# SwiGLU block on one core: the first loads spread over two queues, ten transfers in place of seven

## The chip, the core and the metric

The kernel runs on one core of a Trainium2 chip. The metric is the device time of the launch in microseconds, as the median of several runs. Five engines take part: TensorE (PE; its weight loads are a row of their own, PEld), VectorE (DVE), ScalarE (ACT), GpSimd (POOL) and SyncE (SP). DMA transfers are issued here from two queues, SyncE's and ScalarE's.

## The reference

All arrays are bf16. x has 2048 rows of 640; w_gate and w_up are 640 x 1536; w_down is 1536 x 640.

```
g = silu(x @ w_gate)
u = x @ w_up
out = (g * u) @ w_down
```

## The kernel before, in words

The rows of x are cut into four blocks of 512 (`NSB`, loop over `sb`). The contraction length 640 is five tiles of 128 (`KD`), and the hidden width 1536 is twelve tiles of 128 (`KF`, loop over `fc`). For each block and each `fc` five matmuls make `pg` (gate) and five make `pu` (up), both in PSUM, with the weights as the stationary side and xT, the transposed x, as the moving one (`proj`, line 132). ScalarE takes the Silu of `pg` (line 178), and VectorE multiplies it by `pu` into `aT` (line 179). After twelve `fc` come the products with w_down: `po_t` (line 187) for the last 128 output columns and four `po_a` (line 211) for the first 512, copied out by ScalarE and stored.

TensorE's instructions for the first block's start are kept in the order of the program (`keep_order`). In that order they are: 18 warm-up matmuls on a tile of ones (line 101); transposes of x chunks 0 and 2 (line 123, five each); 4 more warm-up matmuls; transposes of chunks 1 and 3; 2 warm-up matmuls; the gate product of `fc` 0 in two halves (`proj_pair`, line 147: five matmuls for chunks 0 and 2, then five for chunks 1 and 3); the up product of `fc` 0 (line 132); and then everything else. The copies of the transposed chunks into xT (line 128) are VectorE's for chunks 0 and 2; for chunks 1 and 3 ScalarE copies two of the five tiles and VectorE three. So the second half of the gate product waits for copies by both engines. For the blocks after the first, xT is filled by transposing DMAs (line 95).

The weights are loaded in column slices `W_CHUNKS`: slice 0 is `fc` 0 (160 KB for each of gate and up), slice 1 is `fc` 1 and 2 (320 KB each), and three slices of three `fc` follow (480 KB each). The loads are issued at the head of the program (lines 81 to 95):

- SyncE: x chunk 0 (160 KB); x chunks 1 and 3 as one (320 KB); gate slice 1; up slice 1; then the other slices, w_down, and the three transposing loads.
- ScalarE: x chunk 2; gate slice 0; up slice 0; then the load of the function table and a first Silu on one column (line 87), so that the table is there early. ScalarE's xT copies and all later Silus stand behind these.

No queue is written out for the DMAs; each queue issues in the order of the program. Each load signals its end on one of eight completion counters, which are handed out in turn; a load whose counter was used before waits, on its issuing queue, until that earlier load has landed. In the program before, the first eight loads are the two queues' loads down to SyncE's gate slice 2; its up slice 2 is the first that waits, for x chunk 2.

Of the kernel before, what the change touches and what calls it, by code (L numbers as in the profile page):

```python
# [10 lines left out]
def _body(  # L11
# [8 lines left out]
    nc = tc.nc  # L20
# [12 lines left out]
    KD = D // P  # L33
# [7 lines left out]
    W_CHUNKS = [(0, 1), (1, 3), (3, 6), (6, 9), (9, 12)]  # L41
# [10 lines left out]
    x_sb = consts.tile([P, SUB, D], bf16)  # L52
    xT = consts.tile([P, KD, S], bf16)
    wg_sb = consts.tile([P, KD, F], bf16)
    wu_sb = consts.tile([P, KD, F], bf16)
# [5 lines left out]
    x_v = x2.rearrange("(c p) d -> p c d", p=P)  # L61
    xt_v = x2.rearrange("s (kd p) -> s kd p", p=P)
    wg_v = w_gate.rearrange("(kd p) f -> p kd f", p=P)
    wu_v = w_up.rearrange("(kd p) f -> p kd f", p=P)
    wd_v = w_down.rearrange("(kf p) d -> p kf d", p=P)

    def wslice(a, b):
        return slice(a * P, b * P)

    def load_w(eng, dst, src, a, b):  # L70
        eng.dma_start(out=dst[:, :, wslice(a, b)], in_=src[:, :, wslice(a, b)])  # L71

    def load_x(eng, *chunks):
        c_sl = slice(chunks[0], chunks[-1] + 1, 2)
        eng.dma_start(out=x_sb[:, c_sl, :], in_=x_v[:, c_sl, :])  # L75

    ones = consts.tile([P, P], bf16)
    silu_first = consts.tile([P, 1], f32)
    nc.vector.memset(ones[:], 1.0)  # L79

    load_x(nc.sync, 0)
    load_x(nc.scalar, 2)
    load_x(nc.sync, 1, 3)
    load_w(nc.scalar, wg_sb, wg_v, *W_CHUNKS[0])
    load_w(nc.scalar, wu_sb, wu_v, *W_CHUNKS[0])
    load_w(nc.sync, wg_sb, wg_v, *W_CHUNKS[1])
    nc.scalar.activation(silu_first[:], ones[:, 0:1], ACT.Silu)  # L87
    load_w(nc.sync, wu_sb, wu_v, *W_CHUNKS[1])
    for a, b in W_CHUNKS[2:]:
# [65 lines left out]
    for sb in range(NSB):  # L155
        s_sl = slice(sb * S_BLK, (sb + 1) * S_BLK)
        for fc in range(KF):
# [16 lines left out]
            else:  # L174
# [5 lines left out]
                out=aT[:, fc, s_sl], in0=sg[:], in1=pu[:], op=ALU.mult  # L180
# [17 lines left out]
        for q in range(P // Q):  # L198
            nc.scalar.dma_start(
                out=out2[  # L200
                    sb * S_BLK : sb * S_BLK + n_t, DA + q * Q : DA + (q + 1) * Q
                ].rearrange("(i r) c -> r i c", r=Q),
                in_=ot_q[q * Q : (q + 1) * Q, :].rearrange("r (i c) -> r i c", c=Q),
# [106 lines left out]
def kernel(tc, *args):  # L310
    _body(tc, *args)
    tc.close()
    tc.compile()
    _trim(tc.nc)
# [30 lines left out]
```

## Time and profile before

| | us |
|---|---|
| median of 3 runs | 165.53 (165.24 to 165.65) |
| the profiled execution | 165.53 |
| its span in the profile | 164.2 |
| TensorE busy | 160.9 |
| ScalarE busy | 42.5 |
| VectorE busy | 37.9 |

The profile is of one execution; times within it are us from the span's start. In a timeline, a row is a merged run of like instructions: start, length, engine, line, operation, tiles, count, and in brackets how long the engine sat idle before it and what ended that. PEld is the loading of weights, which runs beside the matmuls. SPq and ACTq are the issues of DMAs, not the transfers: a transfer's own time is given as the time from issue to landing. TensorE is busy for nearly all of the span, so the time is that of its work and of the few places where it waits.

The transfers issued first, with the start of the issue and the median time to landing of their kind (us):

| load | queue | issue | to landing |
|---|---|---|---|
| x chunk 0 | SyncE | 0.00 | 2.5 |
| x chunk 2 | ScalarE | 0.13 | 2.7 |
| x chunks 1 and 3 | SyncE | 0.47 | 3.6 |
| gate slice 0 | ScalarE | 0.56 | 4.9 |
| gate slice 1 | SyncE | 0.91 | 5.6 |
| up slice 0 | ScalarE | 1.04 | 6.5 |
| up slice 1 | SyncE | 1.43 | 6.4 |

### The profile page before, as it was taken

Reading aid. Unit: us, or ns where it says so; the run is one execution under the profiler, and the core shown is the slowest. Engines: PE = TensorE matmul, PEld = TensorE weight load, DVE = VectorE, ACT = ScalarE, POOL = GpSimd, SP = SyncE. Lnnn points to the kernel's source line nnn. Section 1 sums busy time; section 2 is a strip of 40 time slices with the busy share of each in tenths; the row PEclk is TensorE's granted clock in tenths of the full one; section 3 lists DMA queues with packets and bytes.
Section 4 is the critical chain, followed back from the end, with each engine's and each line's share of the span. In section 5 each row is a group of like instructions: output and inputs, shape, how many; then the busy total and the mean of one; then the engine's idle time right before and its main releaser. Section 6 shows DMA issues by size and latency. Waiting matters only on the chain.

```text
span 164.2 us, 1881 instructions
## 1 busy us (share of the span) xinstructions
PE 160.9 (98%) x781; PEld 76.0 (46%) x781; DVE 37.9 (23%) x58; ACT 42.5 (26%) x72; POOL 0.6 (0%) x6
## 2 busy tenths in 40 slices
PE   8899999999999999999999999999999999999994
PEld 8544444444444444444444444444444444445442
DVE  2233332230013333221003333322001333332000
ACT  3312222212142222212232222221214222222121
POOL 1000000000000000000000000000000000000000
DMA  7999999704200000002210000000320000000312
GB/s 214 296 327 332 363 192 213 141 0 66 66 32 0 0 0 0 4 0 26 72 56 8 2 4 0 0 0 0 64 68 32 0 0 0 0 0 4 51 37 72
DMA packets 26840, 11.26 MB, mean 69 GB/s; under 512 B 17616, under 2 KB 26832, under 8 KB 26832
## 3 DMA queue, kind: packets, MB, share of 16 engines
q1 hardware_dynamic: 17296, 10.13, 23.1%
q10 hardware_dynamic: 9536, 1.02, 4.2%
q8 instruction: 6, 0.10, 0.3%
q14 instruction: 2, 0.02, 0.0%
HBM read 6.55 MB, written 2.62 MB: 56 GB/s over the span
## 4 chain that ended last, share of the span: by engine, by line
PE 94%; DMA 4%; ACTq 1%; DVE 0%; issue 0%
PE pu L132 32%; PE pg L132 31%; PE po_a L211 25%; PE po_t L187 6%; DMA wu_sb<-in_w_up_dram 4%; PE po_b L224 0%; ACTq L71 0%; ACTq L75 0%; DVE ot_b L232 0%
## 5 line engine op out<-in xcount | busy, mean ns | idle before, releaser
L132 PE MATMUL pu<-xT,wu_sb 128*128 128x512 bf16 x240 | 59.6, 379 | 0.8 <-DMA wu_sb<-in_w_up_dram 0.8
L132 PE MATMUL pg<-xT,wg_sb 128*128 128x512 bf16 x235 | 58.4, 379 | 0.0
L179 DVE TENSOR_TENSOR aT<-sg,pu 128x512 bf16<-128x512 f32 x48 | 33.0, 688 | 101.7 <-PE pu L132 101.7
L178 ACT ACTIVATE sg<-pg 128x512 f32<-128x512 f32 x48 | 28.7, 597 | 72.4 <-PE pg L132 71.0
L211 PE MATMUL po_a<-wd_sb,aT 128*128 128x512 bf16 x192 | 42.1, 379 | 0.0
L132 PEld LDWEIGHTS <-wu_sb 128*128 128x128 bf16 x240 | 23.4, 98 | 29.1 <-DMA wu_sb<-in_w_up_dram 1.1
L132 PEld LDWEIGHTS <-wg_sb 128*128 128x128 bf16 x235 | 23.0, 98 | 27.7
L211 PEld LDWEIGHTS <-aT 128*128 128x128 bf16 x192 | 18.8, 98 | 22.5
L219 ACT CAST ot<-po_a 128x512 bf16<-128x512 f32 x16 | 9.4, 586 | 32.3 <-PE po_a L211 21.2
L187 PE MATMUL po_t<-aT,wd_sb 128*128 128x512 bf16 (+1 forms) x48 | 10.4, 366 | 0.0
L187 PEld LDWEIGHTS <-wd_sb 128*128 128x128 bf16 x48 | 4.7, 98 | 5.1
L196 ACT CAST ot_t<-po_t 128x512 bf16<-128x512 f32 (+1 forms) x4 | 2.2, 559 | 11.7 <-PE po_t L187 11.7
L197 DVE STREAM_TRANSPOSE ot_q<-ot_t 128x512 bf16<-128x512 bf16 (+1 forms) x4 | 2.7, 678 | 9.1 <-ACT ot_t L196 9.1
L101 PE MATMUL pw<-ones 128*128 128x128 bf16 x24 | 3.2, 313 | 0.4 <-DVE ones L79 0.4
L101 PEld LDWEIGHTS <-ones 128*128 128x128 bf16 x24 | 2.6, 147 | 0.4 <-DVE ones L79 0.4
L232 DVE CAST ot_b<-po_b 128x128 bf16<-128x128 f32 x1 | 0.3, 292 | 9.9 <-PE po_b L224 9.9
L128 DVE COPY xT<-pt 128x640 bf16<-128x640 bf16 (+1 forms) x4 | 1.7, 425 | 3.7 <-PE pt L123 3.6
L123 PE MATMUL pt<-ident,x_sb 128*128 128x128 bf16 x20 | 2.5, 311 | 0.0
L123 PEld LDWEIGHTS <-x_sb 128*128 128x128 bf16 x20 | 2.0, 143 | 0.4 <-DMA x_sb<-in_x_dram 0.3
L87 ACT ACT_TABLE_LOAD x1 | 1.3, 1283 | 1.6 <-issue 1.6
L147 PE MATMUL pg<-xT,wg_sb 128*128 128x256 bf16 x10 | 1.3, 281 | 0.0
L128 ACT COPY xT<-pt 128x256 bf16<-128x256 bf16 x2 | 0.7, 372 | 1.5 <-PE pt L123 1.5
(11 smaller groups left out, 3.8 us busy)
## 6 DMA issues: line engine op xcount, KB each, us to landing
out_dram<-ot SPq DMA_DIRECT2D x16, 128.0 KB, 1.7
wd_sb<-in_w_down_dram SPq DMA_DIRECT2D x1, 1920.0 KB, 12.8
wg_sb<-in_w_gate_dram SPq DMA_DIRECT2D x3, 480.0 KB, 7.9
wu_sb<-in_w_up_dram SPq DMA_DIRECT2D x3, 480.0 KB, 8.0
out_dram<-ot_q ACTq DMA_DIRECT2D x12, 32.0 KB, 1.9
x_sb<-in_x_dram SPq DMA_DIRECT2D x1, 320.0 KB, 3.6
wg_sb<-in_w_gate_dram SPq DMA_DIRECT2D x1, 320.0 KB, 5.6
wu_sb<-in_w_up_dram SPq DMA_DIRECT2D x1, 320.0 KB, 6.4
```

What stands on the lines that cost most here:

```text
L87: nc.scalar.activation(silu_first[:], ones[:, 0:1], ACT.Silu)
L101: nc.tensor.matmul(pw[:, 0:P], lhsT=ones[:], rhs=ones[:], start=True, stop=True)
L123: nc.tensor.transpose(out=pt[:, kd - k0, :], in_=x_sb[:, c, kd * P : (kd + 1) * P], identity=ident[:],)
L128: copy(out=xT[:, k0:k1, c_sl], in_=pt[:])
L132: nc.tensor.matmul(ps[:, c0:c1], lhsT=w_sb[:, kd, fc * P : (fc + 1) * P], rhs=xT[:, kd, sb * S_BLK + c0 : sb * S_BLK + c1], start=(kd == 0 ...
L178: nc.scalar.activation(sg[:], pg[:], ACT.Silu)
L179: nc.vector.tensor_tensor(out=aT[:, fc, s_sl], in0=sg[:], in1=pu[:], op=ALU.mult)
L187: nc.tensor.matmul(po_t[:], lhsT=wd_sb[:, kf, DA:D], rhs=aT[:, kf, sb * S_BLK : sb * S_BLK + n_t], start=(kf == 0), stop=(kf == KF - 1),)
L196: nc.scalar.copy(ot_t[:], po_t[:])
L197: nc.vector.transpose(out=ot_q[:], in_=ot_t[:])
L211: nc.tensor.matmul(po_a[:], lhsT=aT[:, kf, s0 : s0 + P], rhs=wd_sb[:, kf, 0:DA], start=(kf == 0), stop=(kf == KF - 1),)
L219: nc.scalar.copy(ot[:], po_a[:])
```

## The change

The first loads are issued as ten transfers in place of seven. Each x chunk is a transfer of its own, chunks 0 and 1 from SyncE and 2 and 3 from ScalarE. Gate slice 0, up slice 0 and gate slice 1 are each cut along the contraction: SyncE loads tiles 0 to 2 of the five, ScalarE tiles 3 and 4. ScalarE's part of gate slice 1 is issued ahead of the function table's load. Up slice 1 and all that follows stay whole and on SyncE. In the built program the order on TensorE, VectorE and GpSimd is the same as before; ScalarE has two DMAs more and SyncE one, and a matmul group that reads a cut slice waits for SyncE's part at its first matmul and for ScalarE's at its fourth.

The counters, in turn, now go round earlier. In the built program SyncE's part of gate slice 1 waits for x chunk 0, ScalarE's part for x chunk 2, SyncE's up slice 1 for x chunk 3, gate slice 2 for x chunk 1, and the next ones for the parts of gate and up slice 0.

```
-    def load_x(eng, *chunks):
-        c_sl = slice(chunks[0], chunks[-1] + 1, 2)
-        eng.dma_start(out=x_sb[:, c_sl, :], in_=x_v[:, c_sl, :])
+    def load_x(eng, c0, c1):
+        eng.dma_start(out=x_sb[:, c0:c1, :], in_=x_v[:, c0:c1, :])
...
-    load_x(nc.sync, 0)
-    load_x(nc.scalar, 2)
-    load_x(nc.sync, 1, 3)
-    load_w(nc.scalar, wg_sb, wg_v, *W_CHUNKS[0])
-    load_w(nc.scalar, wu_sb, wu_v, *W_CHUNKS[0])
-    load_w(nc.sync, wg_sb, wg_v, *W_CHUNKS[1])
+    queues = (nc.sync, nc.scalar)
+    halves = ((0, KD // 2 + 1), (KD // 2 + 1, KD))
+
+    def load_halves(dst, src, a, b):
+        for eng, (k0, k1) in zip(queues, halves):
+            eng.dma_start(out=dst[:, k0:k1, wslice(a, b)], in_=src[:, k0:k1, wslice(a, b)])
+
+    for c in (0, 1):
+        for i, eng in enumerate(queues):
+            load_x(eng, c + 2 * i, c + 2 * i + 1)
+    load_halves(wg_sb, wg_v, *W_CHUNKS[0])
+    load_halves(wu_sb, wu_v, *W_CHUNKS[0])
+    load_halves(wg_sb, wg_v, *W_CHUNKS[1])
     nc.scalar.activation(silu_first[:], ones[:, 0:1], ACT.Silu)
     load_w(nc.sync, wu_sb, wu_v, *W_CHUNKS[1])
```

## The prediction

> **What bounds the kernel now.** First I read the busy shares and the chain of work that ended last on the page. TensorE is busy all through, and the only long piece of the chain that isn't TensorE is one load:
>
> ```profile
> PE 160.9 (98%) x781; PEld 76.0 (46%) x781; DVE 37.9 (23%) x58; ACT 42.5 (26%) x72; POOL 0.6 (0%) x6
> ...
> PE 94%; DMA 4%; ACTq 1%; DVE 0%; issue 0%
> ```
>
> Then the chain in order of time. It enters TensorE at 7.59 us through a transfer of wu_sb issued at 1.04, and from there only matmuls follow, one group of five every 1.08 us to the end of the block:
>
> ```profile
> 1.04 6.51 DMA wu_sb<-in_w_up_dram
> 7.59 1.25 PE pu L132 x5
> 8.84 1.08 PE pg L132 x5
> ```
>
> So the work after 7.59 is fixed by TensorE, and every tenth that its first full "up" group starts earlier comes off the end, as long as no later load becomes late. The change touches nothing but what lies before that. There I read the timeline between 3.5 and 7.7 us; the bracket on the last row is the stall:
>
> ```profile
> 3.56 0.63 PE L101 MATMUL pw<-ones 128*128 128x128 bf16 x4
> ...
> 4.06 1.25 PE L123 MATMUL pt<-ident,x_sb 128*128 128x128 bf16 x10
> 4.49 0.37 ACT L128 COPY xT<-pt 128x256 bf16<-128x256 bf16 x1 [1.38 <-PE pt L123]
> ...
> 5.10 0.42 PE L101 MATMUL pw<-ones 128*128 128x128 bf16 x2
> ...
> 5.47 1.33 PE L147 MATMUL pg<-xT,wg_sb 128*128 128x256 bf16 x10
> ...
> 7.58 0.76 PEld L132 LDWEIGHTS <-wu_sb 128*128 128x128 bf16 x5 [1.06 <-DMA wu_sb<-in_w_up_dram]
> ```
>
> The waits put three stalls of weight loads down to loads: 1.1 us for wu_sb, 0.2 for wg_sb and 0.3 for x chunk 0. Last, what the DMA engines moved (columns: stretch and its length, then busy time and count of the five engines, the granted clock, the DMA share, GB/s):
>
> ```profile
> 1.00:2.00 1.00, 1.00 (x13) 1.00 (x11) 0.00 (x0) 0.39 (x1) 0.00 (x0) 1.00 0.88 228
> 2.00:3.00 1.00, 0.97 (x10) 0.71 (x9) 0.00 (x0) 0.99 (x2) 0.00 (x0) 1.00 1.03 337
> 3.00:4.00 1.00, 1.00 (x12) 0.93 (x9) 0.68 (x2) 0.11 (x1) 0.00 (x0) 1.00 1.09 290
> 4.00:5.00 1.00, 1.00 (x12) 0.94 (x11) 0.49 (x2) 0.37 (x1) 0.00 (x0) 1.00 1.01 282
> 5.00:6.00 1.00, 1.00 (x10) 0.69 (x9) 0.53 (x2) 0.37 (x1) 0.00 (x0) 1.00 1.11 279
> 6.00:7.00 1.00, 0.81 (x8) 0.48 (x5) 0.00 (x0) 0.15 (x1) 0.00 (x0) 1.00 1.14 282
> ```
>
> The engines are full from about 1.4 us on. Summed, they have moved 565 KB by 3.0 us, 855 by 4.0, 1137 by 5.0, 1416 by 6.0 and 1698 by 7.0. Bandwidth is what is short, so the order of the bytes decides.
>
> **The change, part by part.** *Order of the bytes.* Before, SyncE issues the second gate slice (328 KB) at 0.91, ahead of ScalarE's first up slice (164 KB, 1.04), and the second up slice at 1.43. They share the engines, and the first up slice lands at 1.04 + 6.5 = 7.54, when about 1.85 MB are through. After, everything that comes first goes first: x (655 KB), gate slice 0 (819 in all), up slice 0 (983), then gate slice 1 (1311) and up slice 1 (1638). At the rate of before these sums are through at 3.3, 3.9, 4.5, 5.6 and 6.8 us. From bytes to landing I take 0.75 to 1.05 us: x 1 and 3 landed at 0.47 + 3.6 = 4.07 against 3.3, up slice 1 at 1.43 + 6.4 = 7.83 against 6.8. That gives x 4.1, gate 0 4.6 to 4.9, up 0 5.2 to 5.5, gate 1 6.4 to 6.7, up 1 7.6 to 7.8. If ScalarE's part of gate slice 1 (131 KB) is served ahead of SyncE's part of up slice 0, add 0.5 to up 0: 6.0 at worst.
>
> *What TensorE gains.* Slots of the pairs are (1.33 - 0.27)/9 = 0.12 us on average and 0.11 once the first is through; those of transposes and warm-up matmuls (1.25 - 0.31)/9 = 0.10 to 0.11.
> - Up slice 0: the last pair starts at 5.47 + 1.33 - 0.27 = 6.53, so the up group could start at 6.64 instead of 7.59: **0.94**.
> - Gate slice 0: the second of the two warm-up matmuls starts at 5.10 + 0.42 - 0.31 = 5.21, so the first pair could start at 5.31 instead of 5.47: **0.16**.
> - x: the fourth gap matmul starts at 3.56 + 0.63 - 0.31 = 3.88, so chunk 1 could start at 3.98 instead of 4.06: **0.08**. Chunk 3 now has its own load, but TensorE reaches it five slots later, at 4.5.
> - TensorE's slow start takes something back. Weight loads of the transposes take 151 ns (median), those of the pairs 98; only the first pair matmul is slow, 353 ns beside 273. So the array sped up at about 5.6 us, though the granted clock reads 1.00 in every row. With the pairs from 5.23, one more runs at the slow pace: **-0.12**. Bounds: no slow pair, +0.1; all ten slow (twice 0.107 each from 5.23), the up group starts at 7.37 and only 0.22 is left. I take the row's 5.6.
>
> The Trainium skill, page "TensorE: Matmul & The Clock Gate", section "Part 1: The HAM clock gate", says the speed-up comes after a window of about 3.4 us of activity that runs freely, so its place differs from run to run. The trace has one execution and can't show that spread; by the page the last term could lie anywhere between its two ends.
>
> Sum: 0.94 + 0.16 + 0.08 - 0.12 = **1.06 us**; the up group at about 6.5.
>
> *Three more issues, two in front of the table load.* SyncE's issues take 0.40 to 0.53 us each: x 0, x 1, gate 0 and up 0 end at about 1.9, still 2.5 us before their bytes could be served, so they cost nothing. The program has eight completion counters for loads, handed out in turn; a ninth load waits until the first that used its counter has landed. Before, SyncE's second 480 KB load met this, at no cost (SyncE's waits):
>
> ```profile
> SPq L71 <- DMA x_sb<-in_x_dram: 0.3, 1, 0.3
> ```
>
> After, SyncE's part of gate slice 1 waits for x 0 (2.5), up slice 1 for x 3 (about 4.1), the later ones for gate and up slice 0. Behind these waits stand all SyncE loads, w_down and the transposed x loads; w_down landed at 10.68 + 12.8 = 23.5 and is used at 32.6, so they have room. Up slice 1 is needed at 6.5 + 2 x 1.08 = 8.7 and lands at 7.6 to 7.8. Gate slice 1: needed 7.6, lands 6.4 to 6.7.
>
> ScalarE's part of gate slice 1 waits for x 2, which landed at 0.13 + 2.7 = 2.83. Behind it on ScalarE stand the table load (1.28), the first Silu (0.20) and both xT copies (0.37 each), for which the second half of the pairs waits. With an issue of 0.5: 3.35, table to 4.65, Silu to 4.87, copies to 5.25 and 5.63. The second half of the pairs starts at about 5.95, so 0.3 us of cover are left: **0**. The issue is bounded by 0.40 (the shortest) and 2.26 (the longest of SyncE's, its seventh, with four large loads outstanding). ScalarE then has three small ones outstanding, like SyncE's fourth and fifth issue (0.53): I take 0.5. Every tenth over 0.8 would cost a tenth.
>
> The Trainium skill, page "DMA: Bandwidth & Descriptors", section "Rules for kernel authors", speaks against this change: splitting a transfer over two queues buys nothing since both use the same 16 DMA engines, and transfers under 64 KB are mostly overhead (the ScalarE parts are 64 KB). By it alone the gain would be nothing, 165.5. But the rule compares equal bytes; here the row is the wait of 1.06 us for a slice that stood behind 640 KB needed later.
>
> The profiled execution took 165.53 us (span 164.2), which is also the median of the three. 165.53 - 1.06 = 164.47: I say **164.5**, span 163.1. A difference under 0.3% (0.5 us) can't be told from none: faster is under 165.0, slower over 166.0.
>
> **The rivals.**
> - *The array speeds up late.* TensorE becomes the bound of the start. For it: the start is no longer hidden behind the up slice. Against it: 5.6 in this trace. With all pairs slow 0.22 are left: **165.3**.
> - *ScalarE's copies become the wait.* If its issue blocks as SyncE's seventh did (2.26), the table load starts at 5.1, the copies end at 7.4, the second half of the pairs runs 7.44 to 7.99 and the up group starts 0.4 later than now: **165.9**. Slower than before from an issue of 1.86 us on. Against it: three small loads outstanding, not four large ones.
> - *Slower: up slice 1 is late.* It is issued at 4.1 instead of 1.43. If it took its old 6.4 us to land, it would be there at 10.5, 1.8 after its need at 8.7: 164.5 + 1.8 = **166.3**. It turns the gain into a loss once it lands after 9.8. For it: the wait on its counter is new. Against it: most of the 6.4 was queueing behind 1.3 MB, of which all but some 500 KB are gone by 4.1.
> - *No effect.* The first up slice lands at 7.5 whatever stands in front, because the queues are served unevenly: **165.5**. Against it: fewer bytes are in front by 650 KB.
>
> **How the numbers follow.** Forecast (164.1 to 165.0) 0.61, all faster. Late speed-up 0.10, half under 165.0. ScalarE's copies 0.12: 0.01 faster, 0.06 within, 0.05 slower. Up slice 1 late 0.11, slower. No effect 0.06: 0.04 within, 0.02 slower. Together faster 0.67, same 0.15, slower 0.18. Range: at the low end no pair is slow and the second half starts right behind the copies at 5.66, the up group five slots later at 6.2, a gain of 1.4, 164.1, less 0.1 for the scatter of the runs shown: 164.0. The high end, 165.9, leaves out the up-slice case and the worst of ScalarE's. The forecast's own range is 164.1 to 165.0.
>
> **What would show it.** Right: the first full up group starts at 6.4 to 6.7, with no idle in front of weight loads of wu_sb over 0.1; the share of DMA in the chain falls from 4% to under 1% or the chain goes through ScalarE's queue; groups of five follow every 1.08. The table load should stand at about 3.4 and the copies end by 5.7. Wrong: an idle of the pairs' second half with ACT as releaser (ScalarE rival), an idle in front of the second pg or pu group (a late slice 1), pair matmuls of over 340 ns beyond the second (late speed-up), or a wu_sb wait that remains.

## The result, and the profile after

The changed kernel takes 164.50 us (median of 6 runs, 164.34 to 164.80) against 165.59 (165.24 to 166.07) for the kernel before in the same comparison: a ratio of 0.9934, 95% interval 0.9917 to 0.9952. The gain is 1.1 us, or 0.7%, and the interval lies clear of the 0.3% that can't be told from no change. The medians and ranges of the runs below count every execution, and the ratios leave out the few that fell in a slower state (two of twelve with whole slices on two queues, two of ten with up slice 1 late, two of twelve with the order alone and no matmuls between). The profiled execution took 164.52 us, its span is 163.2; before it was 165.53 and 164.2.

The page of the changed kernel first, busy shares and the chain that ended last (from the loads on, line numbers are 6 higher than before):

```profile
PE 160.7 (98%) x781; PEld 76.4 (47%) x781; DVE 37.9 (23%) x58; ACT 42.3 (26%) x72; POOL 0.6 (0%) x6
...
PE 98%; DVE 0%; issue 0%
PE pu L138 32%; PE pg L138 31%; PE po_a L217 25%; PE po_t L193 6%; PE pw L107 2%; PE pt L129 1%; PE pg L153 1%; PE po_b L230 0%; DVE ot_b L238 0%; DVE ones L78 0%
```

TensorE's busy time has hardly moved (160.9 to 160.7 us). What is gone is the 4% of the chain that stood under the load of wu_sb; in its place the chain now runs through TensorE's own start: the warm-up matmuls (pw), the transposes (pt) and the pairs (pg L153). So by this chain the start is bound by TensorE. The timeline of the changed kernel at the start:

```profile
2.43 1.25 PE L129 MATMUL pt<-ident,x_sb 128*128 128x128 bf16 x10
2.80 0.38 ACTq L85 DMA_DIRECT2D wg_sb<-in_w_gate_dram  x1
...
3.20 1.28 ACT L93 ACT_TABLE_LOAD   x1 [3.20 <-DMA x_sb<-in_x_dram]
...
3.90 1.27 PE L129 MATMUL pt<-ident,x_sb 128*128 128x128 bf16 x10
...
4.61 0.66 ACT L134 COPY xT<-pt 128x256 bf16<-128x256 bf16 x2
...
5.18 1.58 PE L153 MATMUL pg<-xT,wg_sb 128*128 128x256 bf16 x10
...
6.49 0.85 PEld L138 LDWEIGHTS <-wu_sb 128*128 128x128 bf16 x5
6.60 1.24 PE L138 MATMUL pu<-xT,wu_sb 128*128 128x512 bf16 x5
...
7.68 1.24 PE L138 MATMUL pg<-xT,wg_sb 128*128 128x512 bf16 x5
```

No bracket stands behind the weight loads of wu_sb any more. The first full up group starts at 6.60 instead of 7.59, and the next group follows 1.08 us later. The times to landing of the cut loads show why (columns: load, queue, count, size, us from issue to landing):

```profile
wg_sb<-in_w_gate_dram SPq DMA_DIRECT2D x1, 96.0 KB, 4.0
wu_sb<-in_w_up_dram SPq DMA_DIRECT2D x1, 96.0 KB, 4.2
wg_sb<-in_w_gate_dram ACTq DMA_DIRECT2D x1, 64.0 KB, 3.7
wu_sb<-in_w_up_dram ACTq DMA_DIRECT2D x1, 64.0 KB, 3.9
```

With issues at 0.91, 1.39, 1.03 and 1.52, gate slice 0 is there at 4.9 and 4.7 and up slice 0 at 5.6 and 5.4, instead of at 5.5 and 7.5.

### The profile page after: what moved, and what is told of

The parts are those of the page before. It is cut to its first block, busy times and chain, and to the rows that moved or that the text cites. A ratio compares the mean times of both kernels' runs of the same rounds, so it can differ in the third digit from the quotient of the medians.

```text
span 163.2 us, 1885 instructions
## 1 busy us (share of the span) xinstructions
PE 160.7 (98%) x781; PEld 76.4 (47%) x781; DVE 37.9 (23%) x58; ACT 42.3 (26%) x72; POOL 0.6 (0%) x6
## 4 chain that ended last, share of the span: by engine, by line
PE 98%; DVE 0%; issue 0%
PE pu L138 32%; PE pg L138 31%; PE po_a L217 25%; PE po_t L193 6%; PE pw L107 2%; PE pt L129 1%; PE pg L153 1%; PE po_b L230 0%; DVE ot_b L238 0%; DVE ones L78 0%
## 5 line engine op out<-in xcount | busy, mean ns | idle before, releaser
L138 PEld LDWEIGHTS <-wg_sb 128*128 128x128 bf16 x235 | 23.0, 98 | 27.7
L153 PE MATMUL pg<-xT,wg_sb 128*128 128x256 bf16 x10 | 1.6, 316 | 0.0
L153 PEld LDWEIGHTS <-wg_sb 128*128 128x128 bf16 x10 | 1.2, 121 | 0.2
```

The lines of the kernel that those rows point to most:

```text
L138: nc.tensor.matmul(ps[:, c0:c1], lhsT=w_sb[:, kd, fc * P : (fc + 1) * P], rhs=xT[:, kd, sb * S_BLK + c0 : sb * S_BLK + c1], start=(kd == 0 ...
L153: nc.tensor.matmul(pair(ps[:]), lhsT=w_sb[:, kd, fc * P : (fc + 1) * P], rhs=pair(xT[:, kd, sb * S_BLK : (sb + 1) * S_BLK]), start=(kd == ...
```

## The experiments

Each is compared with the kernel before, run on the same chip beside it; ratios are to it. The runs were spread over several chips, on which the kernel before has medians from 165.33 to 165.59, so medians of different chips are better compared by their ratios. In all of them TensorE's work after the start is the same, so the time can be read from where the first groups start.

### Is it the order of the bytes, or the cut over two queues?

The order alone: the kernel before, with one load moved, nothing cut.

```
     load_w(nc.scalar, wg_sb, wg_v, *W_CHUNKS[0])
-    load_w(nc.scalar, wu_sb, wu_v, *W_CHUNKS[0])
+    load_w(nc.sync, wu_sb, wu_v, *W_CHUNKS[0])
     load_w(nc.sync, wg_sb, wg_v, *W_CHUNKS[1])
```

> The kernel before with one load moved: up slice 0 is issued whole by SyncE, ahead of gate slice 1, instead of by ScalarE behind gate slice 0. Seven first loads, nothing is cut, no new counter wait. Theory (the order of the bytes carries the gain): about 983 KB stand up to and with up slice 0, through at about 4.5 us at the rate of before, landing 5.2 to 5.6; the first up group starts at 6.6 as in the changed kernel, time 164.5 (164.3 to 164.9). Rival (the cut over both queues carries it): the time stays at the 165.5 of before, with a stall on wu_sb of about 1 us.

Measured: 164.54 us, ratio 0.9951 (0.9932 to 0.9970). One moved line brings as much as the whole change, within what can be told. The timeline of this run, whose profiled execution took 163.96:

```profile
4.92 0.99 PEld L147 LDWEIGHTS <-wg_sb 128*128 128x128 bf16 x10
4.93 1.26 PE L147 MATMUL pg<-xT,wg_sb 128*128 128x256 bf16 x10
5.92 0.85 PEld L132 LDWEIGHTS <-wu_sb 128*128 128x128 bf16 x5
6.03 1.24 PE L132 MATMUL pu<-xT,wu_sb 128*128 128x512 bf16 x5
```

The stall on wu_sb is gone with whole loads too. Here the up group starts even earlier, because in this execution the array was fast ahead of the pairs: they start at 4.93 instead of 5.18, and none of them was slow (1.26 us for ten, against 1.58 above). It is one of the fastest of the ten executions; the median is that of the changed kernel.

The other way round, the cuts without the order: the loads of the changed kernel, up slice 0 behind slice 1.

```
     load_halves(wg_sb, wg_v, *W_CHUNKS[0])
-    load_halves(wu_sb, wu_v, *W_CHUNKS[0])
     load_halves(wg_sb, wg_v, *W_CHUNKS[1])
-    nc.scalar.activation(silu_first[:], ones[:, 0:1], ACT.Silu)
     load_w(nc.sync, wu_sb, wu_v, *W_CHUNKS[1])
+    load_halves(wu_sb, wu_v, *W_CHUNKS[0])
+    nc.scalar.activation(silu_first[:], ones[:, 0:1], ACT.Silu)
```

> The changed kernel with its ten loads and cuts, but up slice 0 (still in two parts) is issued behind gate slice 1 and up slice 1. Theory (order): 1638 KB stand up to and with SyncE's part of up slice 0, which then lands at 7.8 to 8.0 as up slice 1 did; the up group starts at about 8.0 instead of 6.6, time 165.8 to 166.0. Rival (the cut over both queues carries the gain): 164.5 to 164.8.

Measured: 165.87 us, ratio 1.0035 (1.0022 to 1.0049). The stall is back, in the timeline of this run:

```profile
8.14 0.76 PEld L138 LDWEIGHTS <-wu_sb 128*128 128x128 bf16 x5 [1.22 <-DMA wu_sb<-in_w_up_dram]
```

So the order without the cut gives the gain (0.9951, against 0.9934 for the change), and the cut without the order gives none. In both runs the main difference to the kernel they start from is the place of up slice 0, and each moved the time towards what the order says: 165.33 to 164.54, and by the ratios 0.9934 to 1.0035. The second run goes further than the order of before: up slice 0 stands behind up slice 1 too, and its two parts are issued only at 2.97 (ScalarE) and 3.95 (SyncE), behind counter waits. No run has the cuts in exactly the order of before.

### What is the cut for, then?

The next run kept the four x loads and meant to keep the order, with whole slices: gate slice 0 on ScalarE, up slice 0 on SyncE.

```
-    load_halves(wg_sb, wg_v, *W_CHUNKS[0])
-    load_halves(wu_sb, wu_v, *W_CHUNKS[0])
-    load_halves(wg_sb, wg_v, *W_CHUNKS[1])
+    load_w(nc.scalar, wg_sb, wg_v, *W_CHUNKS[0])
+    load_w(nc.sync, wu_sb, wu_v, *W_CHUNKS[0])
+    load_w(nc.sync, wg_sb, wg_v, *W_CHUNKS[1])
```

> The changed kernel's four x loads and its order of the bytes, but gate slice 0 whole on ScalarE, up slice 0 and gate slice 1 whole on SyncE: eight first loads, so that no load up to up slice 1 waits for a counter and ScalarE has no wait in front of its table load. Theory (order is all, the cuts and ScalarE's wait cost and bring nothing): 164.5, the same as the changed kernel and as the run with the order alone; the up group at 6.0 to 6.6 by where the array speeds up. Rival (the counter waits of the changed kernel cost something): 164.2 or below. Rival (cuts even out the DMA engines and bring something): 164.8 or above, with a stall on wg_sb or wu_sb.

Measured: 165.68 us (165.15 to 167.95), ratio 1.0026 (0.9995 to 1.0057): the gain is lost; no execution was under 165.15. That is in the range of the last rival, with its stall on wg_sb; the theory is missed. The waits and the landing times of this run:

```profile
PE pg L153 <- DMA wg_sb<-in_w_gate_dram: 2.0, 1, 2.0
```

```profile
wu_sb<-in_w_up_dram SPq DMA_DIRECT2D x1, 160.0 KB, 5.9
wg_sb<-in_w_gate_dram ACTq DMA_DIRECT2D x1, 160.0 KB, 6.5
```

Gate slice 0, issued by ScalarE at 1.03, took 6.5 us to land, at 7.5, and up slice 0, issued by SyncE at 0.91, landed first, at 6.8. Two things stood against gate slice 0. SyncE's third load was issued 0.12 us earlier than ScalarE's third and was served first. And the trace has 16 completion signals for each load, as many as the core has DMA engines; read as one for each engine, they show single engines behind the others: of gate slice 0, 15 had come by 6.4 and the last at 7.5, and of up slice 0, 15 by 5.2 and the last at 6.8. This execution took 166.58, 0.9 over the median. Without the last signal the pairs could have started 1.1 us earlier, which makes it 165.5, the time of most executions of this run (an estimate; only one has a trace). Two explanations were left: a load loses its place when it is alone on the other queue, or whole slices let single engines fall behind and cuts prevent that. To tell them apart, gate slice 0 went to SyncE too:

```
-    load_w(nc.scalar, wg_sb, wg_v, *W_CHUNKS[0])
+    load_w(nc.sync, wg_sb, wg_v, *W_CHUNKS[0])
```

> As the run with whole slices and four x loads, but gate slice 0 goes to SyncE too: SyncE issues x 0, x 1, gate 0, up 0, gate 1, up 1 in this order, ScalarE only x 2 and x 3. No cut, no counter wait up to up slice 1. Theory (in that run gate slice 0, alone on ScalarE and issued 0.12 us after SyncE's up slice 0, lost its place: a queue keeps its own order, two queues share the engines): gate slice 0 lands at 4.7 to 4.9 and up slice 0 at 5.4 to 5.6, no stall on either, 164.4 (164.0 to 164.9). Rival (whole slices leave single DMA engines behind, and the cuts even them out): gate or up slice 0 still lands after 6, with a stall, 165.0 or above.

Measured: 164.36 us, ratio 0.9932 (0.9910 to 0.9955), the same as the changed kernel, with no cut. Landing times of this run, with issues at 0.91 and later on SyncE:

```profile
wg_sb<-in_w_gate_dram SPq DMA_DIRECT2D x1, 160.0 KB, 3.7
wu_sb<-in_w_up_dram SPq DMA_DIRECT2D x1, 160.0 KB, 3.9
```

Gate slice 0 lands at 4.6 and up slice 0 at 5.3. So on one queue the order was kept with whole slices, and the cut isn't needed for it. Between two queues the place of a line in the program doesn't settle the order: in the run before, gate slice 0 stands ahead of up slice 0 in the program, was issued 0.12 us behind it and landed behind it. To be alone on the other queue is not enough to lose the place, though: in the run with the order alone gate slice 0 is ScalarE's too, but it was issued at 0.56, 0.35 us ahead of up slice 0, and landed ahead of it, at 4.9 against 5.5:

```profile
wg_sb<-in_w_gate_dram ACTq DMA_DIRECT2D x1, 160.0 KB, 4.3
wu_sb<-in_w_up_dram SPq DMA_DIRECT2D x1, 160.0 KB, 4.6
```

The cut in the changed kernel is one way to keep the order (both queues hold the same things in the same order), and one queue for all that must come in order is another. That single engines fall behind is not cured by either: in this run 15 signals of gate slice 1 had come by 6.4 and the last at 7.2, and the group that needs it started at 7.22, 0.3 us after its turn. Why an engine falls behind was not found, nor how much of the loss with whole slices on two queues is due to it.

### ScalarE's place

Up slice 1 was cut like the others, its ScalarE part ahead of the first Silu too, so that ScalarE waits for x chunk 3 before its table load.

```
+    load_halves(wu_sb, wu_v, *W_CHUNKS[1])
     nc.scalar.activation(silu_first[:], ones[:, 0:1], ACT.Silu)
-    load_w(nc.sync, wu_sb, wu_v, *W_CHUNKS[1])
```

> The changed kernel with up slice 1 cut in the same way, its ScalarE part also ahead of the first Silu. That part waits for x chunk 3, which landed at 4.04 in the changed kernel. Theory (the ScalarE path has some cover, then costs one to one): issue 4.04 to 4.42, table load to 5.7, Silu to 5.95, copies to 6.35 and 6.7; the second half of the pairs starts at 6.7 instead of 6.05, the up group at 7.27 instead of 6.60, time 164.5 + 0.67 = 165.2. Rival (ScalarE's place does not matter): 164.5.

Measured: 164.95 us, ratio 0.9978 (0.9964 to 0.9992). The timeline of this run:

```profile
4.29 1.28 ACT L94 ACT_TABLE_LOAD   x1 [4.29 <-DMA x_sb<-in_x_dram]
...
5.70 0.63 ACT L134 COPY xT<-pt 128x256 bf16<-128x256 bf16 x2
...
6.38 0.70 PE L153 MATMUL pg<-xT,wg_sb 128*128 128x256 bf16 x5 [0.71 <-ACT xT L134]
```

The mechanism is the one of the ScalarE rival: the second half of the pairs waits for ScalarE's copies. Whether its size was right can't be told: the median is 0.45 us over the changed kernel's 164.50 on another chip, but by the ratios (0.9978 and 0.9934) it is 0.7, and 0.67 was expected. In this execution the table load began at 4.29, not 4.42, the two copies took 0.63 together and not 0.75, and the array was already fast when the pairs started at 4.95; so the second half's turn was at about 5.5, and it started at 6.38. In the changed kernel itself the copies end at 5.27 and the second half starts at about 6.05 (the last pair at 5.18 + 1.58 - 0.27 = 6.49, less four slots of 0.11), so its cover in that execution is 0.8 us.

### The due time of a later load

Gate slice 2 was issued ahead of up slice 1.

```
+    load_w(nc.sync, wg_sb, wg_v, *W_CHUNKS[2])
     load_w(nc.sync, wu_sb, wu_v, *W_CHUNKS[1])
-    for a, b in W_CHUNKS[2:]:
+    load_w(nc.sync, wu_sb, wu_v, *W_CHUNKS[2])
+    for a, b in W_CHUNKS[3:]:
```

> The changed kernel with gate slice 2 (492 KB, 1.5 us of transfer at 328 GB/s) issued ahead of up slice 1. Theory (each load has a due time, and lateness beyond it adds in full): up slice 1 landed at 7.92 in the changed kernel and is used at 8.65; it lands at about 9.4 and the second up group waits 0.75 us, time 165.2 to 165.3. Rival (later loads are covered whatever their order): 164.5.

Measured: 166.13 us (165.47 to 168.18), ratio 1.0033 (1.0006 to 1.0059). The timeline of this run:

```profile
7.38 1.24 PE L140 MATMUL pg<-xT,wg_sb 128*128 128x512 bf16 x5
...
9.96 0.76 PEld L140 LDWEIGHTS <-wu_sb 128*128 128x128 bf16 x5 [1.83 <-DMA wu_sb<-in_w_up_dram]
9.96 1.25 PE L140 MATMUL pu<-xT,wu_sb 128*128 128x512 bf16 x5 [1.33 <-DMA wu_sb<-in_w_up_dram]
```

Up slice 1 landed at 9.9, not at 9.4, and was wanted earlier than assumed: in this execution the up group started at 6.30, so its due time was 8.46. The group started at 9.96, 1.5 us after its turn. The lateness went into the time, as expected, but it was larger.

### Where the array speeds up

The prediction named the place of the speed-up as a term of the time after the change, and not of the time before, where the stall covered it. Both kernels were run without the 18 warm-up matmuls:

```
-    N_WARM, N_GAP = 18, 4
+    N_WARM, N_GAP = 0, 4
```

For the changed kernel:

> The changed kernel without its first 18 warm-up matmuls, so TensorE has nothing to do until x chunk 0 lands at 2.4. Nothing else is changed. Theory (the place of the speed-up is a term of the time after the change): the array speeds up later than 5.8, all ten pairs run at the slow pace and the up group starts at about 5.18 + 10 x 0.213 = 7.3, perhaps with slow matmuls in it: 165.2 to 165.8, scattering by several tenths. Rival (the start is set by the loads): 164.5.

For the kernel before:

> The kernel before without its first 18 warm-up matmuls. Theory (the stall on up slice 0 covers the slow pace): pairs at the slow pace end at 5.47 + 2.13 = 7.6, just when up slice 0 lands, so nothing is lost unless the array is still slow after 7.6: 165.5 to 166.0, a loss of at most half of what the changed kernel loses. Rival (the warm-up matmuls are worth the same in both kernels): the same loss in both.

Measured: 165.07 us for the changed kernel, ratio 0.9974 (0.9950 to 0.9997), and 165.62 for the kernel before, ratio 0.9995 (0.9973 to 1.0018). The changed kernel loses some 0.6 us by it (from 164.50; by the ratios 0.9934 to 0.9974), a little less than expected (165.2 to 165.8); the kernel before loses nothing that can be told (the same chip's runs of it with the matmuls: 165.43). The pairs in the two profiles (columns: count, shortest, median and longest in ns, first and last start), first the changed kernel without warm-up, then the kernel before without it:

```profile
L153 PE MATMUL pg<-xT,wg_sb x10: 272/297/421, 5.3 to 6.7; 128*128 128x256 bf16 x10
```

```profile
L147 PE MATMUL pg<-xT,wg_sb x10: 273/421/421, 5.5 to 7.3; 128*128 128x256 bf16 x10
```

In the second nearly all pairs are slow and end just when up slice 0 lands: the stall of the weight loads on wu_sb is down from 1.06 to 0.37 us and the time is unchanged. In the changed kernel there is no such stall left to hide them. But not all of its loss is the slow pace: in its profiled execution (164.84) the up group starts at 6.81, 0.21 us later than with the warm-up matmuls, 0.10 of it because gate slice 0 landed later and the pairs start at 5.28 instead of 5.18, and 0.11 in the pairs.

### Do the warm-up matmuls between cost now?

With TensorE on the path from 0.4 us on, by the chain above, the six warm-up matmuls between the transposes and ahead of the pairs stand in it. They were taken out:

```
-                warm(N_GAP)
...
-                warm(2)
```

> The changed kernel without the 4 warm-up matmuls between the transposes and the 2 ahead of the pairs. Theory (TensorE itself is the bound of the start now, so these six slots of 0.107 us are on the path): the transposes of chunk 1 start when it has landed (3.3 to 3.8), the pairs when gate slice 0 has (4.9) instead of at 5.18; at the slow pace half of that is left, so 0.1 to 0.3 us faster than the changed kernel's 164.5: 164.2 to 164.4. Rival (the six matmuls hide in waits for loads): 164.5, no change. Third case (they are what makes the array speed up in time): slower, up to 165.3 as in the late speed-up of the prediction.

Measured: 164.15 us (163.84 to 165.70), ratio 0.9935 (0.9911 to 0.9959). The median is 0.35 lower than the changed kernel's 164.50 on another chip, but the ratio is the same (0.9934 there), so a gain isn't shown. In its profile, whose execution took 163.88, the pairs start at 4.73 instead of 5.18, and the next load is only just in time:

```profile
6.98 1.24 PE L138 MATMUL pg<-xT,wg_sb 128*128 128x512 bf16 x5
...
8.10 0.76 PEld L138 LDWEIGHTS <-wu_sb 128*128 128x128 bf16 x5 [0.37 <-DMA wu_sb<-in_w_up_dram]
8.10 1.25 PE L138 MATMUL pu<-xT,wu_sb 128*128 128x512 bf16 x5
```

The weight loads, which run ahead of the matmuls, stood 0.37 us for up slice 1; the group itself started 0.04 us after its turn (6.98 + 1.08 = 8.06). The same edit on the kernel with one queue:

> The same, without the 4 and 2 warm-up matmuls between the transposes and ahead of the pairs. If order is all and the six slots are on the path, as they were worth 0.3 us in the changed kernel: 164.0 to 164.2, the pairs from 4.7 to 4.9. If the single queue leaves a stall: as the run beside it, 165.0 or above.

Measured: 164.29 us, ratio 0.9933 (0.9914 to 0.9951); without the edit it was 164.36. The median falls short of the 164.0 to 164.2 expected. And on the kernel with the order alone:

> The kernel before with up slice 0 moved to SyncE ahead of gate slice 1 (the first run), without the 4 and 2 warm-up matmuls. x chunks 1 and 3 as one load land at 4.1, where the transposes of chunk 1 started anyhow (4.17), so the 4 gain nothing and only the 2 ahead of the pairs can: at most 0.2 us, 164.3 to 164.5. Rival (all six slots count): 164.1 or below.

Measured: 164.22 us (163.77 to 166.31), ratio 0.9944 (0.9914 to 0.9974), between what the theory (164.3 to 164.5) and the rival (164.1 or below) say, and the scatter leaves it open. Beside them on that chip stood the changed kernel as it is:

> The changed kernel as it is, beside the three others on one chip, for its place among them and its scatter: 164.5, with runs from 164.1 to 165.0 by where the array speeds up (4.5 to 6.5 us).

Measured: 164.34 us (163.98 to 164.92), ratio 0.9937 (0.9915 to 0.9958). So none of these versions can be told from the changed kernel; all lie 0.6 to 0.7% under the kernel before. What can stop an early start is in the waits of the changed kernel's second profiled execution, which took 164.91:

```profile
PE pu L138 <- DMA wu_sb<-in_w_up_dram: 1.0, 1, 1.0
```

In this execution the array sped up early, ahead of the second transposes, no pair was slow, and up slice 1 was wanted at about 8.0; its last two completion signals came at 9.0 and 9.1, 1.2 us after the other fourteen. That is the rival "up slice 1 is late", in one execution of the changed kernel, at a price of about 1.1 us (the group started at 9.10). In that execution the early start gained nothing, because the last signals of the next load came late; whether that also holds the other versions back, the one trace of each doesn't show.

## Why the prediction was right

The forecast was 164.5 us with the up group at about 6.5, a span of 163.1 and a gain of 1.06; measured were 164.50, 6.60 and 163.2, and the profiled execution gained 1.01.

- *Order of the bytes.* Right, and shown by experiments in both directions. Landings forecast and measured (us): x by 4.1, and 4.0; gate slice 0 at 4.6 to 4.9, and 4.9; up slice 0 at 5.2 to 5.5 (6.0 at worst), and 5.4 and 5.6; gate slice 1 at 6.4 to 6.7, and 6.4 and 6.6; up slice 1 at 7.6 to 7.8, and 7.9. The sums of bytes against the rate of before came within 0.1 us.
- *Up slice 0, 0.94, and gate slice 0, 0.16.* Right: both waits are gone from the profile.
- *x, 0.08.* Came out at 0.16: the transposes of chunk 1 start at 3.90 instead of 4.06, because chunk 0 also landed 0.09 earlier (first transpose at 2.43, before 2.52). The prediction took chunk 0 as unchanged. Gate slice 0 and x together moved the pairs from 5.47 to 5.18, by 0.29, where 0.24 was forecast.
- *The slow pace, -0.12.* Mis-sized: about -0.25. From the first pair to the up group it is 6.60 - 5.18 = 1.42 us, where the profile of before gives 6.64 - 5.47 = 1.17 without the stall and the prediction added 0.12; three pairs ran at the slow pace (slots of 0.21) where it had two. With the terms above, 0.94 + 0.29 - 0.25 = 0.98, and the measured shift of the up group is 7.59 - 6.60 = 0.99. So two misses of opposite sign, 0.05 and 0.13, partly cancel. That the array sped up near the 5.6 us of the one trace was luck of this execution: in the other it did so at 3.7. The bound for an early speed-up, +0.1, counted the pairs alone; with transposes at the fast pace too, the up group started at about 5.8 there.
- *ScalarE's wait, 0.* Right, with more cover than worked out: its issue took 0.38, not 0.5, the table load stood at 3.20 (3.35 forecast) and the copies ended at 5.27 (5.63). A second wait in the same place made it cost. The cover is that of an execution with slow pairs: in the second profiled one the copies ended at 5.21 and the second half started at 5.26, so with an early speed-up ScalarE's copies are next to the bound.
- *Counter waits on SyncE, 0.* Right in the profiled execution: SyncE stood 0.5 us for x chunk 0 and 1.3 for x chunk 3, in its waits, with no stall behind. In another execution up slice 1 was late by its last two signals; whether its late issue had a part in that was not tried apart. Two readings beside this were wrong, at no cost to the sum. Counted alike, the change makes eleven loads of seven down to up slice 1, four more and not three, and two of the four are SyncE's. And w_down is first used by weight loads at 32.2, not 32.6.
- *The rule against the change.* The Trainium skill, page "DMA: Bandwidth & Descriptors", section "Rules for kernel authors", says that spreading transfers over queues brings nothing since they share the engines. The runs agree for the cut itself: it brought nothing in the run without the order (1.0035), and the order without the cut brought the gain (0.9951, and 0.9932 on one queue). The prediction was right to weigh the bytes ahead of a load above the rule, but it credited the change as a whole; the part that matters is one moved load.

The rivals: a late speed-up is real as a term (0.6 us without the warm-up), but was not the case here. ScalarE's copies became the wait with a second wait added, and by less than 0.1 us in the profile without the matmuls between, where the second half started at 5.36, right behind the copies' end at 5.31. "Up slice 1 is late" came true in one of two profiled executions, by a late last signal. "No effect" is excluded.

## What to carry to other kernels

When the engines of a start-up phase are full, add up the bytes that stand ahead of each load and compare their time with the time at which the load is wanted: a small load behind large ones that are wanted later is worth moving, and a single line can do it. Keep what must land in order on one queue, or give both queues the same things in the same order; a load that is issued later on the other queue can lose its place (here a lag of 0.12 us was enough in the one trace). Once a stall is gone, look at what it covered: here TensorE's slow first microseconds in one execution, and the last signals of the next load in another.

## What the runs showed that had not been expected

- The place where the array speeds up differs between executions, and the granted clock in the profile (1.00 throughout) doesn't show it: by the lengths of the matmuls it lay at 3.7 us in one execution of the changed kernel, at 5.8 in the other, at 6.1 in the changed kernel without its first warm-up matmuls and at 7.1 in the kernel before without them. The Trainium skill, page "TensorE: Matmul & The Clock Gate", section "Part 1: The HAM clock gate", says that the window of activity after which the speed-up comes runs freely, so its place shifts from run to run. The runs show such a shift, 2.1 us between two executions of the same kernel; they don't show the window itself.
- Single executions differ by more than the gain. The order alone ran from 163.84 to 165.19 in ten executions; beside it on the same chip the kernel before ran from 164.73 to 166.88 in 32 of 33. The place of the speed-up and the late signals can account for part of that, but the runs don't separate them.
- A load is as late as its last completion signal: 15 of 16 by 6.4 us and the last at 7.5 for gate slice 0 with whole slices on two queues, 14 by 7.8 and the last two at 9.0 and 9.1 for up slice 1 in the changed kernel's second profiled execution.
